# Handing out D^T G one step after the transposes of D in a fused attention, MoE and soft-MoE kernel

## The chip, the cores and the metric

One core of a Trainium2 chip runs the whole program. The metric is device time in microseconds (us), from the start of the program on the core to its end; the median of several runs counts. The profile is that of one execution. It names the engines PE (TensorE, matmuls; PEld is its weight load), DVE (VectorE), ACT (ScalarE), POOL (GpSimd) and SP (SyncE, which here issues the transfers).

## What is computed

Chunked attention, then a squared-relu MLP, then a soft mixture of eight experts, all in float32:

```python
# q, k, v: 8 x 8 x 576 x 64, cut into chunks of 64 rows
attn = softmax(scale * q_c @ k_c.T); x = attn @ v_c     # x: 4608 x 512
h = np.maximum(x @ w_in, 0.0)                           # 4608 x 2048
x = h * h @ w_out                                       # 4608 x 512
logits = x @ phi                                        # 4608 x 32
d = softmax of logits down the 4608 tokens
slot_input = d.T @ x                                    # 32 x 512
slot_out = per expert: relu(slot_input[e] @ w1[e]) @ w2[e]
c = softmax of logits along the 32 slots
return c @ slot_out                                     # 4608 x 512
```

## The kernel before

The 4608 tokens are 36 tiles of 128, grouped into blocks: blocks 0 and 1 with one and two tiles (joined for the later work as "block 1"), and blocks 2 to 12 with three tiles each. A block's work in the middle of the kernel is 16 **steps**, one for each 128 columns of w_in. In step t TensorE computes h for this step (`moe_h`, L727, 12 matmuls), ScalarE takes relu and square, and two steps later (`LAG = 2`) TensorE transposes the result g (`moe_turn`, L761), ScalarE copies it into a buffer G (`moe_keep`, a copy at L188), and after every fourth step TensorE adds to the logits L (`moe_logits`, L778). The transposes of g go to one of two PSUM banks in turn: `gT` for even steps, `L0` for odd ones, once block 2's logits are done.

w_out is applied late: the kernel keeps G, the squared activations with tokens down the partitions, and computes D^T G, where D is the exponential of the logits in the softmax over tokens, with a running maximum. This is the work of `soft(b)`, a generator that starts in the step after the block's last logits. Each `yield` ends its part in one step; `run_gen` puts the next part into the next step. Since a block's last logits fall into step 1 of the block behind it, its parts fall into these steps of the next block:

- step 2: Ls, the logits scaled (L854)
- step 3: their sum over four partial rows (L864)
- step 4: the running maximum, the exponential dts (L874 to L883)
- step 5: `slots_softmax`, the softmax over slots (L896 to L907)
- step 6: the transposes of D (L917, TensorE) and, on VectorE, dd = their product with a scale (L919)
- step 7: D^T G, 24 matmuls of dd with the four G buffers of the block (L926), and on VectorE `acc = acc * al + y` (L937)

Into the same steps `put_until` puts the attention of later tiles, each operation by its stage. Of what stands around step 7 and 8 it is this: in step 8 the scores of the block's third tile (L446 to L448, then on VectorE their maximum L452 and the subtraction L455) and the sum for the scales of another tile (`reduce`, L205 and L206, from three row maxima `am`, L182); in step 9 the product with v of the second tile (L498 to L500). Within a step TensorE's order is attention, h, the part of soft, the transposes of g, the logits.

TensorE executes in this written order (`ST_ORDER = ("PE",)`). For the other engines and for SP the order is made by a scheduler that simulates the program when it is built; each engine's queue then runs in that order.

Buffers that matter here: `misc()` hands out three PSUM banks in turn in the order of the calls, to scores, sums, products with v and the parts of soft alike; a bank can be written anew when its last reader is done. G has a ring of seven buffers (`NG_RING`), taken in the order of first use, four for each block. dd has one buffer. In block 12 the buffers of G that are idle by then are given to the loads of the expert weights at step 9 (`at(u0 + 9, ...)`), and `load_units` issues these loads on SP.

Of the kernel before, what the change touches and what calls it, by code (L numbers as in the profile page):

```python
# [74 lines left out]
def kernel(  # L75
# [95 lines left out]
    def misc():  # L171
        x = bank_of.get(turn[0])
        if x is None:
            while n_misc[0] % 3 in held_banks:
                n_misc[0] += 1
            x = n_misc[0] % 3
            n_misc[0] += 1
        return ps_m.tile([P, 512], F32, tag=f"misc{x}", name="misc")
# [670 lines left out]
    def soft(b):  # L849
        s0, n = blocks[NB if b == 1 else b]  # L850
        last = s0 + n == NT
# [68 lines left out]
            out=dd, in0=tp, in1=iv.unsqueeze(2).to_broadcast([P, n, NS]), op=ALU.mult  # L920
        )
        yield
        y = misc()
        for j in range(n):
            for g in range(NQ):
# [408 lines left out]
    for i in range(9, NT):  # L1334
        b, j = tile_block[i]
# [51 lines left out]
    end = len(steps) + LAG  # L1387
    at(2, lambda: put_rest(2, [("s", NB, x) for x in range(fa, NF)]))
    run_gen(2, soft(1))
    t = min(0, min(slots, default=0))  # L1390
    ctx.enter_context(
        tc.manual_schedule(engines={getattr(mybir.EngineType, e) for e in ST_ORDER})
    )
    while t < end or any(x >= t for x in slots):
        put_rest(t)
        put_until(t + 1)
        b, f = steps[t] if 0 <= t < len(steps) else (None, None)
        if b == 2 and f % QF == 0:
            put_rest(t, [("s", NB, x) for x in range(f, f + QF)])
        if b is not None:  # L1400
            moe_h(b, f)
            moe_relu(b, f)
            moe_square(b, f)
            if (b, f) == (NB - 1, NF - 1):
                give((big, f"xb{b % 2}", 1536))
        for fn in slots.pop(t, []):
            fn()
        if b == NB - 1 and f % 2:
            give((big, f"wi{f // 2}", 1024))
        if 0 <= t - LAG < len(steps):  # L1410
            b, f = steps[t - LAG]
            moe_turn(b, f)
            moe_keep(b, f)
            if f % QF == QF - 1:
                moe_logits(b, f // QF)
            if f == NF - 1:
                if b == NB - 1:
                    give((big, "g0", 1536))
                gen = soft(b)
                run_gen(t + 1 if b < NB - 1 else t, gen)  # L1420
                if b == NB - 1:
                    slots[t].pop()()
        t += 1
# [220 lines left out]
```

## Time and profile before

| | us |
|---|---|
| runs (three) | 777.81, 778.6, 783.45 |
| median of the runs | 778.6 |
| the profiled execution | 778.18 |
| its span in the profile | 776.4 |
| TensorE busy | 707.2 (91%) |
| ScalarE busy | 457.1 (59%) |
| VectorE busy | 431.7 (56%) |
| GpSimd busy | 167.4 (22%) |

The span reaches from the first to the last instruction of the profile. Busy time is the union of an engine's instructions. A wait is idle time of an engine ahead of an instruction, put down to the instruction or transfer that released it.

### The profile page before, as it was taken

The numbers are of one execution on the slowest core, as the hardware profiler recorded it, in microseconds if no ns is written. First come the engines' busy times: TensorE is split into PE (matmuls) and PEld (weight loads), VectorE is DVE, ScalarE is ACT, GpSimd is POOL, SyncE is SP. The second block draws the span as 40 slices with busy tenths as digits, with TensorE's granted clock in tenths as the row PEclk, the third lists the DMA queues.
The fourth block names the chain that finished last, engine by engine and source line by source line (L and its number), as shares of the span: only waits on it lengthen the run. The fifth ranks groups of instructions, "written<-read, shape, count | busy, mean of one in ns | idle before, by whom it ended". The sixth has DMA issues, their size and how long they took to land.

```text
span 776.4 us, 16693 instructions
## 1 busy us (share of the span) xinstructions
PE 707.2 (91%) x6612; PEld 456.1 (59%) x6612; DVE 431.7 (56%) x908; ACT 457.1 (59%) x951; POOL 167.4 (22%) x209
## 2 busy tenths in 40 slices
PE   5788999889999999998999989999999999969790
PEld 4677776665566565665666656656566565524350
DVE  4799996367666565656566566656565301022160
ACT  3688887554666565656676556656566655531150
POOL 3332211131223222223122222322232200030000
PEclk9899999999999999999999999999999999999995
DMA  7896934234364544543544737444567423669998
GB/s 155 215 279 161 217 120 139 66 66 87 81 137 92 98 83 83 123 96 69 109 96 89 100 62 142 86 96 83 82 90 184 150 83 117 227 214 356 349 353 255
DMA packets 242589, 110.47 MB, mean 142 GB/s; under 512 B 201808, under 2 KB 235600, under 8 KB 242512
## 3 DMA queue, kind: packets, MB, share of 16 engines
q1 hardware_dynamic: 242512, 109.41, 58.0%
q8 instruction: 52, 0.85, 0.5%
q14 instruction: 25, 0.20, 0.1%
HBM read 78.71 MB, written 9.44 MB: 114 GB/s over the span
## 4 chain that ended last, share of the span: by engine, by line
PE 65%; DMA 14%; DVE 12%; ACT 3%; issue 2%; SPq 1%; POOL 1%; DVEq 0%; POOLq 0%; ACTq 0%
PE hps L727 38%; PE gT L761 7%; PE L L778 4%; PE misc L926 4%; DMA unit<-in_moe_w_dram 3%; DMA qkT<-qk 3%; DMA qkv<-in_v_dram 2%; PE ehps L1466 2%; DVE qk L276 2%; DMA qkv<-in_q_dram 2%; DMA qkv<-in_k_dram 2%; DMA pT<-p 1%; DVE am L182 1%; DVE vbd L425 1%; DVE stage L281 1%
## 5 line engine op out<-in xcount | busy, mean ns | idle before, releaser
L727 PE MATMUL hps<-xb,wi 128*128 128x384 f16 (+2 forms) x2400 | 407.8, 320 | 0.5 <-ACT g L742 0.2
L727 PEld LDWEIGHTS <-wi 128*128 128x128 f16 x2400 | 224.9, 98 | 138.8 <-issue 17.6
L742 ACT ACTIVATE g<-hps,inv_w 128x384 f32<-128x384 f32 (+1 forms) x200 | 112.7, 563 | 98.4 <-PE hps L727 96.6
L188 ACT ACTIVATE G<-gT 128x384 f32<-128x384 f32 (+1 forms) x200 | 94.2, 471 | 33.8 <-PE gT L761 30.6
L182 DVE TENSOR_REDUCE am<-qkv 128x1 bf16<-128x512 f32 x90 | 61.9, 687 | 83.6 <-DMA qkv<-in_v_dram 31.9
L761 PE MATMUL gT<-ident,g 128*128 128x128 f32 x576 | 98.1, 277 | 4.0 <-ACT G L188 3.1
L749 ACT ACTIVATE g<-g 128x384 f32<-128x384 f32 (+2 forms) x188 | 96.8, 515 | 1.5
L761 PEld LDWEIGHTS gT<-ident,g 128*128 128x128 f32 x576 | 73.0, 144 | 28.8 <-issue 10.4
L420 POOL TENSOR_SCALAR vbd<-qkv,as 64x512 f16<-64x512 f32 x54 | 41.7, 772 | 97.2 <-PE misc L500 81.5
L471 POOL TENSOR_TENSOR ex<-ex,rs 128x512 f32<-128x512 f32 x27 | 29.3, 1085 | 103.4 <-DVE rs L468 93.0
L410 DVE SCALAR_TENSOR_TENSOR qk<-qkv,as,qk 128x512 f16<-128x512 f32 x54 | 39.4, 756 | 20.8 <-ACT qk L405 20.3
L425 DVE SCALAR_TENSOR_TENSOR vbd<-qkv,as,vbd 64x512 f16<-64x512 f32 x54 | 47.3, 876 | 1.0
L405 ACT ACTIVATE qk<-qkv,as 128x512 f16<-128x512 f32 x54 | 36.8, 716 | 10.7 <-DVE as L215 10.7
L778 PE MATMUL L<-g,wp 128*32 128x384 f32 x384 | 41.7, 498 | 0.0
L926 PE MATMUL misc<-G,dd 128*32 128x512 f32 x288 | 33.4, 596 | 7.2 <-DVE dd L919 6.6
L484 POOL TENSOR_TENSOR p<-ex,p 128x512 f16<-128x512 f32 x27 | 34.9, 1292 | 21.7 <-ACT p L481 21.7
L481 ACT ACTIVATE p<-ex 128x512 f16<-128x512 f32 x27 | 17.0, 630 | 35.5 <-POOL ex L471 35.5
L223 POOL TENSOR_SCALAR iv_all<-ai 128x1 f32<-128x1 f32 x27 | 7.5, 276 | 118.5 <-DVE ai L218 117.6
L435 DVE COPY qbd<-qkT 64x1024 f16<-64x1024 f16 x54 | 22.7, 420 | 17.3 <-DMA qkT<-qk 16.5
L510 DVE SCALAR_TENSOR_TENSOR xb<-misc,xb 128x512 f16<-128x512 f32 x27 | 18.1, 671 | 25.1 <-ACT xb L504 24.8
L461 ACT ACTIVATE ex<-ex,es 128x512 f32<-128x512 f32 x27 | 19.4, 718 | 19.4 <-DVE ex L455 19.4
L854 DVE TENSOR_TENSOR Ls<-L,iv_all 128x384 f32<-128x384 f32 x12 | 6.6, 553 | 41.0 <-PE L L778 40.8
(156 smaller groups left out, 1018.7 us busy)
## 6 DMA issues: line engine op xcount, KB each, us to landing
unit<-in_moe_w_dram SPq DMA_DIRECT2D x34, 512.0 KB, 4.5
unit<-in_moe_w_dram SPq DMA_DIRECT2D x60, 256.0 KB, 6.0
qkv<-in_q_dram SPq DMA_DIRECT2D x72, 128.0 KB, 3.4
qkv<-in_k_dram SPq DMA_DIRECT2D x72, 128.0 KB, 3.3
qkv<-in_v_dram SPq DMA_DIRECT2D x72, 128.0 KB, 3.4
stage<-in_moe_w_in_dram SPq DMA_DIRECT2D x16, 512.0 KB, 5.1
stage<-in_moe_w_out_dram SPq DMA_DIRECT2D x16, 512.0 KB, 5.8
out_dram<-o SPq DMA_DIRECT2D x14, 512.0 KB, 6.3
```

The lines of the kernel that those rows point to most:

```text
L182: dve.tensor_reduce(out=am, in_=src, axis=AX.X, op=ALU.max, apply_absolute_value=True)
L188: act.activation(out=out, in_=in_, func=ACTF.Copy)
L405: act.activation(out=qk16[:, 2 * a], in_=flat[:, a], func=ACTF.Copy, scale=v["s"][:, a : a + 1])
L410: dve.scalar_tensor_tensor(out=qk16[:, 2 * a + 1], in0=flat[:, a], scalar=v["s"][:, a : a + 1], in1=qk16[:, 2 * a], op0=ALU.mult, op1=ALU. ...
L420: pool.tensor_scalar(out=dst[0], in0=vin, scalar1=v["s"][pr, 2:3], scalar2=1.0, op0=ALU.mult, op1=ALU.mult,)
L425: dve.scalar_tensor_tensor(out=dst[1], in0=vin, scalar=v["s"][pr, 2:3], in1=dst[0], op0=ALU.mult, op1=ALU.subtract,)
L727: pe.matmul(hp, wi[f][:, wl, kt], xb[:, xl, kt], start=(nm == 0), stop=(nm == 3 * KT - 1))
L742: act.activation(out=g, in_=hp, func=ACTF.Relu, scale=sc)
L749: act.activation(out=g, in_=g, func=ACTF.Square)
L761: pe.transpose(gt_ps[b, f][:, j], g[:, j * P : (j + 1) * P], ident)
L778: pe.matmul(L_ps[g0][NS * x : NS * x + NS, :n], wp[:, QF * q + x], g[:, x, :n], start=(q == 0), stop=(q == NQ - 1), tile_position=(0, NS * x),
L926: pe.matmul(y[NS * g : NS * g + NS], dd[:, j], G_q[b, g][:, j], start=(j == 0), stop=(j == n - 1), tile_position=(0, NS * g), skip_group_c ...
```

## The change

After the transposes of D, `soft` gives up one more step before it hands out D^T G, for every block but block 1 and the last. D^T G and the acc behind it fall into step 8 of the next block, and what else is in steps 7 and 8 stays where it is. The last part of the generator comes one step later as well; it is empty.

```diff
@@ -920,6 +920,8 @@
             out=dd, in0=tp, in1=iv.unsqueeze(2).to_broadcast([P, n, NS]), op=ALU.mult
         )
         yield
+        if not last and b > 1:
+            yield
         y = misc()
         for j in range(n):
             for g in range(NQ):
```

## Rows read from the trace of the kernel before

**Rows 1.** The page: busy us (share) and instructions; busy tenths in forty slices.

```profile
PE 707.2 (91%) x6612; PEld 456.1 (59%) x6612; DVE 431.7 (56%) x908; ACT 457.1 (59%) x951; POOL 167.4 (22%) x209
...
PE   5788999889999999998999989999999999969790
```

**Rows 2.** TensorE's waits: line waited for, us in total, times, longest.

```profile
PE misc L926 <- DVE dd L919: 6.6, 4, 2.0
...
PE gT L761 <- ACT G L188: 3.1, 3, 1.8
```

**Rows 3.** TensorE's timeline (start, length, instruction, [idle before]): D^T G, three blocks.

```profile
457.67 2.78 PE L926 MATMUL misc<-G,dd 128*32 128x512 f32 x24 [1.89 <-DVE dd L919]
...
507.55 2.78 PE L926 MATMUL misc<-G,dd 128*32 128x512 f32 x24 [0.88 <-DVE dd L919]
...
558.33 2.78 PE L926 MATMUL misc<-G,dd 128*32 128x512 f32 x24 [1.79 <-DVE dd L919]
```

**Rows 4.** TensorE's timeline around D^T G of one block, 351 to 363 us.

```profile
351.57 0.37 PE L917 MATMUL misc<-ident,dts 32*128 32x32 f32 x3
351.98 0.55 PE L761 MATMUL gT<-ident,g 128*128 128x128 f32 x3
352.64 2.11 PE L727 MATMUL hps<-xb,wi 128*128 128x384 f16 x12
356.79 2.78 PE L926 MATMUL misc<-G,dd 128*32 128x512 f32 x24 [2.05 <-DVE dd L919]
359.51 0.55 PE L761 MATMUL gT<-ident,g 128*128 128x128 f32 x3
...
360.59 0.17 PE L205 MATMUL misc<-am,ones 128*128 128x3 bf16 x1
...
360.64 2.11 PE L727 MATMUL hps<-xb,wi 128*128 128x384 f16 x12
362.59 0.49 PE L761 MATMUL gT<-ident,g 128*128 128x128 f32 x3
362.92 0.19 PE L498 MATMUL misc<-pT,vbd 128*128 128x64 f16 x1
```

**Rows 5.** VectorE's timeline of the same block, 335 to 363 us.

```profile
335.23 0.69 DVE L182 TENSOR_REDUCE am<-qkv 128x1 bf16<-128x512 f32 x1 [0.33 <-DMA qkv<-in_v_dram]
...
348.88 0.42 DVE L435 COPY qbd<-qkT 64x1024 f16<-64x1024 f16 x1
349.34 0.69 DVE L510 SCALAR_TENSOR_TENSOR xb<-misc,xb 128x512 f16<-128x512 f32 x1
...
352.83 0.26 DVE L900 TENSOR_TENSOR cmat<-misc,cm 128x96 f32<-128x96 f32 x1
355.02 0.69 DVE L182 TENSOR_REDUCE am<-qkv 128x1 bf16<-128x512 f32 x1 [1.93 <-DMA qkv<-in_v_dram]
...
356.49 0.25 DVE L919 TENSOR_TENSOR dd<-misc,iv_all 128x96 f32<-128x96 f32 x1
359.64 0.75 DVE L937 SCALAR_TENSOR_TENSOR acc<-acc,al,misc 128x512 f32<-128x512 f32 x1 [2.90 <-PE misc L926]
360.79 0.69 DVE L452 TENSOR_REDUCE mx<-misc 128x8 f32<-128x512 f32 x1 [0.40 <-PE misc L206]
...
361.53 0.68 DVE L455 TENSOR_TENSOR ex<-misc,mx 128x512 f32<-128x512 f32 x1
```

**Rows 6.** TensorE's timeline at block 1's D^T G.

```profile
178.05 2.78 PE L926 MATMUL misc<-G,dd 128*32 128x512 f32 x24
181.39 0.55 PE L761 MATMUL gT<-ident,g 128*128 128x128 f32 x3 [0.56 <-ACT G L188]
```

**Rows 7.** ScalarE's timeline after block 2's D^T G.

```profile
209.12 0.99 ACT L188 ACTIVATE G<-gT 128x384 f32<-128x384 f32 x2 [1.64 <-PE misc L926]
```

**Rows 8.** Stretches: length, busy (instructions) by engine, clock, DMA share, GB/s.

```profile
660.00:670.00 10.00, 10.00 (x70) 6.25 (x69) 0.00 (x0) 5.49 (x13) 0.00 (x0) 1.00 0.76 270
...
680.00:690.00 10.00, 6.37 (x49) 3.44 (x49) 3.04 (x10) 4.02 (x9) 3.69 (x4) 1.00 0.23 78
```

## The prediction

> **What bounds the kernel now.** I read the page first: its busy shares and its forty slices [rows 1]. TensorE is busy 91% of the span, and its slices stand at 9 nearly without a break from the tenth on; VectorE, the next engine for this change, is busy 56%. The reader is to see a kernel whose middle, about 190 to 675 us, goes at the pace of TensorE's own instruction stream, so only TensorE's idle time can be won there. So I went next to TensorE's waits, longest in total first [rows 2]. The first line is the very instruction that the change moves: the 24 matmuls of D^T G (L926) waited for dd (L919) four times, 6.6 us in all, at most 2.0. The other wait that I need is that of the transposes of g for the copy into G (L761 for L188), 3.1 us in three times.
>
> Then the order of time. TensorE's timeline through one block [rows 4] shows a waiting case: the transposes of D (L917) at 351.57, those of g, the h of step 7, which ends at 354.74, and then nothing until D^T G starts at 356.79, 2.05 late. The other three cases waited 1.89, 0.88 and 1.79 [rows 3]; with the 2.05 that is 6.61. The other six of the ten blocks that the edit touches have no such row: there dd came just in time.
>
> VectorE's timeline of the same block says why dd was late [rows 5]. dd is a short instruction (0.25 us), and its input was there since about 352. But it stands behind a row maximum of v (L182), which waited 1.93 for a transfer until 355.02, and behind the rest of slots_softmax (0.78, from the maximum's end at 355.71 to 356.49). That maximum belongs to a later tile; VectorE's order comes from the scheduler, so a maximum whose load is late holds up whatever stands behind it. After dd VectorE idles 2.90 until D^T G is done and acc (L937) can be added.
>
> **The change part by part.** Nothing is added or removed on any engine: ten times the 24 matmuls and the acc behind them come one step later, and the part issues no transfer. The terms:
>
> *1. The wait for dd.* In the new order TensorE goes from the end of h at 354.74 to the transposes of g, the scores of the next block's third tile, the sum for its scales (L205), the next h, and only then to D^T G. Between the end of D^T G and the end of that h stand today 359.51 to 360.64 (1.13) and 360.64 to 362.59 (1.95) [rows 4], 3.08 together. So D^T G would come at 357.82, and dd ends at 356.74 [rows 5]: 1.08 to spare in the worst of the four cases, more in the others. Term: -6.61.
>
> *2. What is reached earlier.* In those four blocks the scores come up to 2.05 and 2.72 (the length of D^T G, 356.79 to 359.51) earlier than today. Is anything of theirs late? The scores need qbd, whose second copy started at 348.88 and took 0.42; the sum needs three maxima, the last of which was taken at 335.23 [rows 5], twenty microseconds before. Both would be reached after 354.74. Cost 0; without that cover it would be the lateness of either.
>
> *3. The banks.* misc() hands out three banks in turn. Today the order is D^T G, scores, sum, then the p v product of the second tile (L498); after the change it is scores, sum, D^T G, p v. The scores inherit the bank that xl (L510) had left at 350.03, the sum that of slots_softmax, left by L900 at 353.09, D^T G that of the transposes of D, which dd itself has read. The p v product had the bank of D^T G, free once acc has read it; now it has that of the scores, free once L455 has read it. In the new order L452 can start right after dd, at 356.74, and L452 and L455 together took 360.79 to 362.21, 1.42 [rows 5]: free at 358.16. TensorE comes to p v at 357.82 + 2.72 + 0.33 (362.59 to 362.92 today [rows 4]) = 360.87. Cost 0, with 2.71 to spare; what it costs without that cover is the second rival.
>
> *4. The ring of G.* G has seven buffers, handed out in the order of first use. From the third block on, a block's D^T G is read long before its buffers come round: the first reuse is by the copy of step 14 of the next block. In the block after block 2 it is otherwise: the two early groups filled the ring in another order, and that block's second buffer is the first one of block 2. So its copy at step 6 must wait for block 2's D^T G. The trace has this today: the copy waited for the end of L926 and ran at 209.12 [rows 7]. Today no transpose waits for it, since D^T G comes before the transposes that use the other gT bank. One step later the transposes behind D^T G (step 8) need the bank that this copy empties. The same pattern is in the trace once, behind block 1's D^T G: it ended at 180.83, and the transposes started at 181.39, after 0.56 of waiting for the copy [rows 6]. Below, the cost is nothing; above, the two copies in a row, 0.99 [rows 7]. I take 0.56, since that row is the same sequence. Term: +0.56, once. ScalarE's queue is held at that copy some 3 us longer than today, and a relu may stand behind the two copies; TensorE needs that relu's bank only for the second h after D^T G, so at least one h of 1.95 and a p v product lie between, and I put it at 0.
>
> *5. The end.* In the last block the loads of expert weights into the three idle G buffers wait for block 11's D^T G; there it moves by a transpose and an h, some 2.3 us. These loads go through SP in order. The DMA engines have room: 0.76 busy at 660 to 670, 0.23 at 680 to 690 [rows 8], 7.7 idle microseconds in the last of these alone. Cost 0; if the room were not there, 2.3.
>
> A rule of the Trainium skill speaks against term 1: the page "Perfetto Trace Analysis", section Optimization Strategy, takes a gap that repeats on the engine that should be saturated as a possible sign of too few buffers. By that rule the gap would come back at another instruction and the sum would be the time before, as in rival three below. The trace agrees only in part: the gap ends on dd, long after the bank of D^T G was left at 350.03, and shows in four blocks of ten [rows 2, 5].
>
> **Sum.** The profiled execution took 778.18, 1.8 more than its span of 776.4. 778.18 - 6.61 + 0.56 = 772.13. The median of the runs before is 778.6, 0.4 above the profiled execution, so I put 772.5. Bounds of the known terms: 771.9 (no cost of the ring) to 773.0 (0.99 there).
>
> **The rivals.**
>
> *One: dd is later too.* VectorE's order is made anew, and another instruction that waits for a load may come to stand ahead of dd. If that costs one more 1.93 [rows 5], 1.08 of it is covered in the worst blocks and 0.85 is seen; in four blocks 3.4 comes back: 776. For it: such maxima wait often. Against it: up to dd nothing in a block is moved.
>
> *Two, the other side: acc stands in the way.* Today acc follows dd directly on VectorE. If it kept that place, VectorE would stand still from dd until D^T G has ended at 357.82 + 2.72 = 360.54, acc would start 0.13 later as today (359.51 to 359.64 [rows 4, 5]) and take 0.75, then L452 and L455 1.42: the bank of p v would be free at 362.84 and not at 358.16, and TensorE, there at 360.87, would wait 2.0. Nine blocks have this p v: 18 us, 790.5. It decides from 0.7 us a block (6.05 over nine), which is when L452 starts more than 3.4 us after dd. Against it: VectorE's order follows what is ready first (a maximum ran twenty microseconds before the sum that needs it [rows 4, 5]), and the scores will be done by 355.82 (354.74 and 1.08, from 359.51 to 360.59 today [rows 4]), 4.7 us before D^T G has ended.
>
> The rule beside it is in the Trainium skill, page "PSUM — Partial Sum Buffer", section Engine vs sequencer instructions: VectorE's and ScalarE's queues are strictly first in, first out. By it whatever stands behind a waiting acc does wait; the trace agrees, with 2.90 of idle VectorE ahead of acc.
>
> *Three: the wait only moves*, in whole, to another instruction that VectorE is late with, or the order of the other engines changes so that as much is lost elsewhere: 778.6, no change. Against it: I found nothing late behind D^T G.
>
> **How the numbers follow.** Forecast, 772.5: 0.70. One, 776: 0.12. Two, 790.5: 0.07. Three, 778.6: 0.07. The rest, 0.04, is a new order that saves more than the four waits. The forecast's own spread is about 1 us each way, and a measurement of this kernel can tell about 1% from no change, that is below 770.8 or above 786.4. So the gain of 0.8% that I expect lies inside "within 1%"; part of the forecast's spread and the rest lie beyond it. Faster by over 1%: 0.14; within 1%: 0.78; slower: 0.08. The range takes in one and three and leaves out two: 770.0 to 779.5. The forecast alone would be 771.0 to 774.0.
>
> **What would show it.** In the changed kernel's profile: no wait of L926 for dd in TensorE's waits (right) or one of a microsecond in several blocks (rival one). On VectorE L452 and L455 between dd and acc (right) or acc directly behind dd and waits of L498 (rival two). One new wait of L761 for the copy at about 212, around 0.5. A wait of scores or sum for VectorE would refute term 2, and a start of the last phase that is not some 6 us earlier would refute the sum, as would any wait of over a microsecond that is repeated from block to block.

## The result: 1.1% faster

The changed kernel took 771.66 us (median of six runs, 769.53 to 774.87); the kernel before, in the runs beside it, 779.95 (six runs, 777.16 to 784.92). The ratio is 0.9892, with a 95% interval of 0.9861 to 0.9923. 772.5 was predicted. The profile after is of an execution of 774.87, the slowest of the six, with a span of 773.1.

The page of the changed kernel shows nearly the same busy times as [rows 1]; TensorE's is 3.9 higher at a mean granted clock of 0.972 (0.982 before), and none of that lies in the middle of the kernel, as the rows of the first experiment show:

```profile
PE 711.1 (92%) x6612; PEld 457.7 (59%) x6612; DVE 428.1 (55%) x908; ACT 457.3 (59%) x951; POOL 161.9 (21%) x209
...
PE   5788999898999999999999999999999999969790
```

The difference is in TensorE's waits (line waited for, us in total, times, longest). The line of [rows 2] in which D^T G, now L928, waits for dd is gone; the one wait of L928 that is left is in the last block, which the edit leaves out. The waits of the transposes of g have one more case:

```profile
PE gT L761 <- ACT G L188: 3.7, 4, 1.9
...
PE misc L928 <- DVE rs__8963 L936: 0.5, 1, 0.5
```

TensorE's timeline through the block of [rows 4] has no gap. Behind the h of step 7 come the transposes of g, scores and sum, the next h, then D^T G:

```profile
353.05 0.37 PE L917 MATMUL misc<-ident,dts 32*128 32x32 f32 x3
353.44 0.55 PE L761 MATMUL gT<-ident,g 128*128 128x128 f32 x3
354.09 2.11 PE L727 MATMUL hps<-xb,wi 128*128 128x384 f16 x12
356.03 0.49 PE L761 MATMUL gT<-ident,g 128*128 128x128 f32 x3
357.06 0.17 PE L205 MATMUL misc<-am,ones 128*128 128x3 bf16 x1
...
357.12 2.11 PE L727 MATMUL hps<-xb,wi 128*128 128x384 f16 x12
359.15 2.78 PE L928 MATMUL misc<-G,dd 128*32 128x512 f32 x24
361.87 0.55 PE L761 MATMUL gT<-ident,g 128*128 128x128 f32 x3
362.25 0.19 PE L498 MATMUL misc<-pT,vbd 128*128 128x64 f16 x1
```

VectorE's timeline of this block, to compare with [rows 5]: the maximum still waits for its load, 1.74, and dd still ends late, at 358.00. But D^T G starts only at 359.15, so 1.15 are to spare (1.08 were worked out). L452 and L455 run between dd and acc, which waits no more:

```profile
356.28 0.69 DVE L182 TENSOR_REDUCE am<-qkv 128x1 bf16<-128x512 f32 x1 [1.74 <-DMA qkv<-in_v_dram]
...
357.75 0.25 DVE L919 TENSOR_TENSOR dd<-misc,iv_all 128x96 f32<-128x96 f32 x1
357.92 0.68 DVE L452 TENSOR_REDUCE mx<-misc 128x8 f32<-128x512 f32 x1
...
358.65 0.68 DVE L455 TENSOR_TENSOR ex<-misc,mx 128x512 f32<-128x512 f32 x1
...
362.01 0.75 DVE L939 SCALAR_TENSOR_TENSOR acc<-acc,al,misc 128x512 f32<-128x512 f32 x1
```

The one new wait stands behind block 2's D^T G, in TensorE's timeline:

```profile
210.63 2.78 PE L928 MATMUL misc<-G,dd 128*32 128x512 f32 x24
213.97 0.55 PE L761 MATMUL gT<-ident,g 128*128 128x128 f32 x3 [0.56 <-ACT G L188]
```

### The profile page after: what moved, and what is told of

Same layout as the page of the kernel before. It is cut to its first block, busy times and chain, and to the rows that moved or that the text cites. A ratio compares the mean times of both kernels' runs of the same rounds, so it can differ in the third digit from the quotient of the medians.

```text
span 773.1 us, 16704 instructions
## 1 busy us (share of the span) xinstructions
PE 711.1 (92%) x6612; PEld 457.7 (59%) x6612; DVE 428.1 (55%) x908; ACT 457.3 (59%) x951; POOL 161.9 (21%) x209
## 4 chain that ended last, share of the span: by engine, by line
PE 71%; DMA 10%; DVE 9%; ACT 4%; issue 1%; POOL 1%; SPq 1%; DVEq 0%; POOLq 0%; ACTq 0%
PE hps L727 41%; PE gT L761 7%; PE misc L928 4%; PE L L778 4%; DMA unit<-in_moe_w_dram 3%; PE ehps L1468 2%; DVE qk L276 2%; DMA qkT<-qk 2%; DMA qkv<-in_k_dram 2%; DMA qkv<-in_q_dram 1%; PE misc L332 1%; DMA qkv<-in_v_dram 1%; DVE stage L281 1%; PE misc L498 1%; DVE qk L275 1%
## 5 line engine op out<-in xcount | busy, mean ns | idle before, releaser
L420 POOL TENSOR_SCALAR vbd<-qkv,as 64x512 f16<-64x512 f32 x54 | 37.2, 689 | 87.5 <-PE misc L500 71.8
L425 DVE SCALAR_TENSOR_TENSOR vbd<-qkv,as,vbd 64x512 f16<-64x512 f32 x54 | 44.7, 828 | 0.7
L928 PE MATMUL misc<-G,dd 128*32 128x512 f32 x288 | 35.1, 622 | 0.5 <-DVE rs__8963 L936 0.5
```

Of the source, the lines that this page charges most:

```text
L420: pool.tensor_scalar(out=dst[0], in0=vin, scalar1=v["s"][pr, 2:3], scalar2=1.0, op0=ALU.mult, op1=ALU.mult,)
L425: dve.scalar_tensor_tensor(out=dst[1], in0=vin, scalar=v["s"][pr, 2:3], in1=dst[0], op0=ALU.mult, op1=ALU.subtract,)
L928: pe.matmul(y[NS * g : NS * g + NS], dd[:, j], G_q[b, g][:, j], start=(j == 0), stop=(j == n - 1), tile_position=(0, NS * g), skip_group_c ...
```

## The experiments

The theory: the gain is the waits for dd, less the new wait behind block 2. The first rival: there is a gain in every block, from VectorE no longer standing still ahead of acc. For the stretch in which the two differ I take the *middle*, from the start of block 1's D^T G to the start of the last block's transposes of D (178.05 to 684.91 before: 506.86). Two of the expectations below begin it at block 2's D^T G, but that one is moved by the edit itself.

### The same kernel again

No edit.

> The changed kernel once more, beside the kernel before on the same chip. Theory (the gain is the four waits for dd, 6.6 us, less the one new wait behind block 2's D^T G, 0.56): 6 us faster, ratio 0.9925; in the profile no wait of D^T G for dd, the middle (from block 2's D^T G to the last transposes of D) 6 to 7 us shorter. Rival (there is a gain in every block, from VectorE no longer standing still ahead of acc): 8 to 10 us faster, ratio 0.989 or lower, and the blocks without a wait are shorter too, by 0.2 us or more each.

Median 771.96, ratio 0.9891 (0.9857 to 0.9925). No wait for dd in its profile; the middle took 499.26, against 498.84 in the first profile of the change: 7.6 and 8.0 less than the 506.86 before. That is more than the 6 to 7 of the theory, and the ratio is the rival's.

The middle as one stretch (length, busy by engine, granted clock, DMA share, GB/s), in the first profile before and then in the first of the change:

```profile
178.05:684.91 506.86, 492.62 (x4444) 308.54 (x4444) 278.18 (x611) 313.45 (x664) 115.30 (x136) 1.00 0.50 106
```

```profile
180.95:679.79 498.84, 492.09 (x4444) 308.41 (x4443) 273.23 (x607) 314.01 (x664) 110.78 (x135) 1.00 0.50 107
```

TensorE is busy 0.5 less than before; its idle time fell from 14.24 to 6.75, which is 7.5 of the 8.0.

### Only the four blocks that waited, and only the other six

```diff
-        if not last and b > 1:
+        if not last and b in (5, 7, 8, 9):
```

> The later D^T G only in the four blocks that waited before (5, 7, 8 and 9). Theory: the whole of the gain and no wait behind block 2's D^T G: 6.6 us faster, ratio 0.9915. Rival (a gain in every block alike): four tenths of it, about 3 us, ratio 0.996.

```diff
-        if not last and b > 1:
+        if not last and b in (2, 3, 4, 6, 10, 11):
```

> The later D^T G only in the other six blocks (2, 3, 4, 6, 10 and 11). Theory: no gain, and 0.56 us lost behind block 2's D^T G: ratio 1.000 to 1.001; the four waits for dd stand in the profile as before, about 6.6 us in all. Rival (a gain in every block alike): six tenths of it, about 5 us, ratio 0.994.

The four alone: 772.89, ratio 0.9905 (0.9876 to 0.9935), nearly all of the gain. The other six: 780.13, ratio 1.001 (0.9988 to 1.0031), nothing. Their lines in TensorE's waits, first that of the six, then that of the four:

```profile
PE misc L928 <- DVE dd L919: 6.0, 4, 1.8
```

```profile
PE misc L928 <- DVE dd L919: 0.3, 1, 0.3
```

With the six moved the four waits stand where they stood. A gain in every block alike is out: it would have given the six 0.994.

### Block 2 left out

```diff
-        if not last and b > 1:
+        if not last and b > 2:
```

> The later D^T G in all blocks from block 3 on; block 2 as before. Theory: as the changed kernel without the wait of the transposes of g for the copy behind block 2's D^T G, so 0.56 us faster than it in the profile's middle: ratio to before 0.9915. Rival (that wait comes from something other than the ring of G): the wait of 0.56 at about 214 us stays.

Median 771.52, ratio 0.9893 (0.9863 to 0.9922). The wait of the transposes for the copy behind block 2's D^T G is gone, and with it one case of four and 0.7 of the total:

```profile
PE gT L761 <- ACT G L188: 3.0, 3, 1.7
```

So the wait does come from the ring of G. In the time 0.56 can't be told from nothing: the interval is over 4 us wide. The middle, 498.52, is 0.3 and 0.7 below the two profiles of the change.

### dd made later

```diff
-        dve.tensor_tensor(
-            out=dd, in0=tp, in1=iv.unsqueeze(2).to_broadcast([P, n, NS]), op=ALU.mult
-        )
+        for _ in range(5 if not last and b > 1 else 1):
+            dve.tensor_tensor(
+                out=dd, in0=tp, in1=iv.unsqueeze(2).to_broadcast([P, n, NS]), op=ALU.mult
+            )
```

In the kernel before, five times:

> The kernel before with dd computed five times over in the blocks from 2 on (four more instructions of 0.25 us on VectorE ahead of D^T G, the same values). Theory (D^T G comes just when dd is done): each extra 0.7 to 1.0 us is seen in full in the blocks where dd had nothing to spare, eight of ten: 6 to 8 us slower than before, ratio 1.008 to 1.010, and the waits for dd sum to 12 to 15 us. Rival (the waits for dd are a sign of something else that is late): no slower.

In the changed kernel, five times, and nine times with 9 in place of 5:

> The changed kernel with dd computed five times over. Theory: in the changed kernel dd ends 1.0 us or more ahead of D^T G in every block, so the 0.7 to 1.0 us are covered: as the changed kernel, ratio to before 0.990, and no waits for dd over 0.1 us. Rival (VectorE is what sets the pace around D^T G): slower than the changed kernel by what dd costs more, 8 us, ratio 1.000.

> The changed kernel with dd computed nine times over, 1.5 to 2.0 us more. Theory: more than the three tightest blocks have to spare (1.0, 1.15 and 1.22 us), less than the others have (2.3 and more): waits for dd of 0.3 to 1.0 us in three blocks, 1 to 3 us in all, ratio to before 0.992 to 0.994. Rival (VectorE sets the pace): 15 us slower than the changed kernel, ratio 1.01.

Before, the delay is seen: 792.29, ratio 1.0157 (1.0109 to 1.0206). After, the same delay is nearly covered: 773.45, ratio to before 0.9924 (0.99 to 0.9948), with one wait for dd, of 0.2; the middle took 500.32, some 1.3 more than in the changed kernel, and the transposes of D waited once more for the exponential, 0.8. Nine times is more than the cover: 777.2, ratio 0.9969 (0.9943 to 0.9994). The waits of the kernel before with five and of the changed kernel with nine:

```profile
PE misc L927 <- DVE dd L920: 16.6, 8, 3.3
```

```profile
PE misc L929 <- DVE dd L920: 5.0, 5, 1.2
```

Two sizes were off. With nine, five blocks wait and not three, and they wait 5.0 us in all where 1 to 3 were expected: the nine dd together took 2.58, one takes 0.25, so the delay was 2.3 and not 1.5 to 2.0. And the kernel before with five lost 13.7 us where 6 to 8 were expected. The waits rose by 10.0 (6.6 to 16.6; the five dd together took 1.42, so the delay was 1.2 and not 0.7 to 1.0), and something was added to them: after the longest wait, 3.30, the 24 matmuls of D^T G took 4.48 and not 2.78, in TensorE's timeline; and the row of the stretch from 361 to 364 (length, busy by engine, granted clock, DMA share, GB/s) has the clock at 0.56, which is the lower of its two levels, 1.2 GHz, for most of the stretch:

```profile
360.57 4.48 PE L927 MATMUL misc<-G,dd 128*32 128x512 f32 x24 [3.30 <-DVE dd L920]
```

```profile
361.00:364.00 3.00, 3.00 (x20) 0.78 (x16) 0.00 (x0) 0.00 (x0) 0.00 (x0) 0.56 0.00 0
```

That profile has three such stretches in its middle, each after a wait for dd (3.30, 2.48 and 3.27). Their D^T G took 4.48, 4.40 and 4.48, 5.0 more than three times 2.78; with the 10.0 that is 15.0, and the middle grew by 14.8 (521.66 for 506.86).

### Two steps later

```diff
-        if not last and b > 1:
+        if not last and b > 2:
             yield
+            yield
```

> D^T G two steps later instead of one, in the blocks from 3 on, block 2 as before. Theory: nothing is left to gain, the waits for dd being gone with one step: the same as one step later without block 2, ratio 0.989 to 0.992. Rival (more room, more gain): another 3 us or more, ratio 0.986 or lower.

Median 772.99, ratio 0.9915 (0.9887 to 0.9942): nothing more than with one step.

### slots_softmax out of the way

```diff
-        if not last:
+        early = last or b == 1
+        if not last and early:
             slots_softmax(misc()[:, : n * NS])
+        if not last:
             yield
...
             out=acc, in0=acc, scalar=al, in1=y, op0=ALU.mult, op1=ALU.add
         )
+        if not early:
+            yield
+            slots_softmax(misc()[:, : n * NS])
```

(The step that slots_softmax had stays, empty.)

> The kernel before with D^T G where it was, in step 7, but slots_softmax moved from step 5 to the step behind D^T G in the blocks from 2 on, so that its instructions no longer stand between the late maximum and dd on VectorE. Theory (dd is late by the load that the maximum waits for, 1.9 us, and by the rest of slots_softmax behind it, 0.8): the four waits shrink by about 0.8 us each, from 6.6 to 3 to 4 us in all; ratio 0.995 to 0.997. Rival (dd is late by its own input, or by what is ahead of the maximum): the waits stay, ratio 1.000.

Median 779.02, ratio 0.9981 (0.9957 to 1.0005), nearly nothing, where the theory had 0.995 to 0.997. On VectorE dd now stands directly behind the late maximum:

```profile
355.62 0.69 DVE L182 TENSOR_REDUCE am<-qkv 128x1 bf16<-128x512 f32 x1 [2.09 <-DMA qkv<-in_v_dram]
356.22 0.25 DVE L921 TENSOR_TENSOR dd<-misc,iv_all 128x96 f32<-128x96 f32 x1
```

D^T G waits 0.89 in this block where it waited 2.05, but 5.2 in all, in six blocks, and not the 3 to 4 expected. And the transposes of D now wait for the exponential in three blocks more than before, as here, and give part of the gain back:

```profile
352.47 0.37 PE L919 MATMUL misc<-ident,dts 32*128 32x32 f32 x3 [0.72 <-ACT dts L877]
...
356.52 1.92 PE L928 MATMUL misc<-G,dd 128*32 128x512 f32 x16 [0.89 <-DVE dd L921]
```

In this block the load that comes late is the larger part of dd's lateness, as the rows said; shortening the chain behind it isn't enough. No run took the maximum itself, or its load, out of dd's way.

### The kernel before, three more profiles

The open point after the first experiments was the size: 6.6 of waits removed, but 7.4 to 8.3 gained. The second rival: the first profile showed fewer waits than an execution has.

> The kernel before once more, for a second profile. Theory (the gain is the waits for dd that one execution shows): waits for dd in the same four blocks, 6 to 7 us in all, the middle (from block 2's D^T G on) within 0.5 us of the first profile's. Rival (the first profile showed fewer waits than an execution has on average, which is why the gain by the median is over 6 us): 8 us or more of waits.

> The kernel before, a third profile. Theory (dd's lateness differs between executions, since it hangs on when loads arrive; the first profile, 6.6 us in four blocks, was a low one): the waits for dd sum to 7 to 9 us in six blocks or more, the middle 2 to 4 us longer than in the first profile. Rival (the second profile was the odd one): 6 to 7 us in the same four blocks.

> The kernel before, a fourth profile, on the same terms: 7 to 9 us of waits for dd in six blocks or more by the theory, 6 to 7 us in the same four blocks by the rival.

Beside more runs of the same kernel the second stands at 782.17, ratio 1.0017 (0.9982 to 1.0052); the third and the fourth are single executions, of 780.66 and 776.55. The second, third and fourth profile of the kernel before have these lines among TensorE's waits, where [rows 2] has 6.6 in four cases:

```profile
PE misc L926 <- DVE dd L919: 8.0, 7, 2.1
```

```profile
PE misc L926 <- DVE dd L919: 8.6, 7, 2.1
```

```profile
PE misc L926 <- DVE dd L919: 7.1, 6, 1.9
```

The mean of the four is 7.6; the first was the lowest. And in two of the four, after the longest wait, D^T G ran at the lower clock. The second profile's timeline with its stretch from 460 to 464, and below it the third's with its stretch from 457 to 461; the granted clock is 0.58 in both:

```profile
460.60 4.48 PE L926 MATMUL misc<-G,dd 128*32 128x512 f32 x24 [2.11 <-DVE dd L919]
```

```profile
460.00:464.00 4.00, 3.40 (x17) 0.82 (x21) 0.51 (x3) 0.00 (x0) 0.00 (x0) 0.58 0.01 4
```

```profile
456.43 4.22 PE L926 MATMUL misc<-G,dd 128*32 128x512 f32 x24 [2.12 <-DVE dd L919]
```

```profile
457.00:461.00 4.00, 4.00 (x26) 1.00 (x17) 0.30 (x1) 0.00 (x0) 0.00 (x0) 0.58 0.02 4
```

The first profile, with waits of up to 2.05, kept the full clock there, and so did the fourth, with up to 1.89. Neither profile of the changed kernel has such a stretch between the two ends of its middle. The middles of the four are 506.86, 510.50, 507.76 and 505.94, 507.8 in the mean; those of the change 498.84 and 499.26, 499.1. The difference is 8.7. The waits came as the theory of these runs had them, the middles did not: the third was to be 2 to 4 longer than the first and is 0.9 longer, and the fourth is 0.9 shorter.

## Why the prediction came out as it did

**The wait for dd (term 1)** was the right mechanism: the four blocks alone bring the gain, the other six nothing, and a dd made later costs 13.7 before and hardly anything after. Its size is what was off: -6.61 was read from one execution. The prediction takes dd as just in time in the other six blocks. In the first profile that holds for four of them, blocks 2, 3, 4 and 6, where D^T G starts 0.05 to 0.13 behind the end of dd; blocks 10 and 11 have 1.09 and 2.06 to spare. A load that comes a little later makes a wait out of the first kind: blocks 3, 4 and 6 are the three more that wait in the second and the third profile. The maximum ahead of dd waited 1.66, 1.57 and 1.83 for its load there in the first profile, and 1.85, 1.75 and 2.38 in the second. By four profiles the waits are 7.6 in the mean, and 1.7 and 1.44 more at the lower clock in two of the four, 0.8 in the mean: 8.4. With the 0.56 against it that makes 7.8. From 779.95, the median of the kernel before beside the result, it leads to 772.1, from 779.37, beside the repeat, to 771.6; measured were 771.66 and 771.96. The price of a wait was taken as its length; that a long one can slow the work behind it was not in the sum.

That 772.5 lies as near as 0.8 to the measured 771.66 is in part luck. The forecast gain was 6.1, the measured one 8.3; of the 2.2 between them 1.35 was made up by the start, since the sum began at 778.6 and the kernel before took 779.95 in the runs beside the result.

**What is reached earlier, and the banks (terms 2 and 3)** cost nothing that was seen, as worked out. Neither scores nor sum wait for VectorE in the blocks that were moved (a sum waits for its maximum at 185.01, 0.50, in the second profile of the change, and at 188.08, 0.81, in the first before, both ahead of block 2's D^T G). The one p v product that waits for L455, 0.16 at 437.87 in the second profile, stands 32 us behind block 6's D^T G and not next to it. L455 ended at 359.33 (358.65 and 0.68), 2.92 ahead of the p v product at 362.25; 2.71 had been worked out.

**The ring of G (term 4)** was right to the digit: one wait, 0.56, at 213.97, and with block 2 left out it is gone. It was read from the same sequence at block 1 [rows 6].

**The end (term 5)**: block 11's D^T G moved by a transpose and an h, and the last phase took no longer for it that could be seen: from the last transposes of D to the end of the span 91.5 in the second profile of the change and 91.5 in the first before. In the first profile of the change it took 93.3, of which 1.7 is the last block's D^T G at the lower clock (4.48). The room for the loads stands in [rows 8].

**The start of the last phase**, to be some 6 us earlier: the last transposes of D start at 679.79 and 674.54, 5.1 and 10.4 earlier than before. Most of that spread lies ahead of the first block that was moved, since block 1's D^T G started at 180.95 and 175.28 (178.05 before); from there on it is 8.0 and 7.6.

**Rival one** (dd later too) did not come: the smallest room between dd and its D^T G in the changed kernel's two profiles is 1.01 and 1.30. **Rival two** (acc in the way) did not come: in VectorE's new order acc stands behind L452, L455 and eight more, which fits the argument that this order follows what is ready first. What it would have cost wasn't tried. **Rival three** (the wait only moves) is what happened in part where slots_softmax was moved instead, not here. The rule of the Trainium skill, page "Perfetto Trace Analysis", section Optimization Strategy, that a repeated gap may mean too few buffers, did not hold for this gap: it was gone with one step and no buffer more.

The **chances** put 0.78 on "within 1%"; the measured 1.1% lies just beyond, with an interval on both sides of the line. That follows in the main from the size of term 1.

About 0.9 of the 8.7 in the middle is in no term (8.4 - 0.56 = 7.8). TensorE's other listed waits there sum to 7.24, 7.90, 5.14 and 6.71 in the four profiles before and, without the new 0.56, to 5.69 and 6.47 in the two after: 0.7 less in the mean, but they differ by more than that between executions of one kernel, so it stays open.

## What to carry to other kernels

Where one engine sets the pace in a written order, put other work between a hand-over and its user when the hand-over hangs on something that arrives at uneven times; one step was enough here, and two brought no more. Read a wait that hangs on transfers from more than one execution before it is used as a term, and look at the matmuls behind it: a long wait can also cost clock. Before a user is moved, go through every ring that it holds; the only cost here was found by counting seven buffers.

## What the runs showed of the hardware that I had not expected

After a wait of 2.11, 2.12 or 3.30 us of a TensorE that had been busy, the granted clock fell to its lower level while the next matmuls ran, and 24 matmuls that take 2.78 took 4.48, 4.22 and 4.48. After the waits for dd of up to 2.05 in the four profiles of the kernel before it stayed up. But the length of the wait doesn't settle it. Ahead of the middle, in the first profile of the change, the clock fell after a wait of 1.55; TensorE's timeline and the stretch from 177 to 179:

```profile
175.54 1.33 PE L661 MATMUL misc<-pT,vbd 128*64 128x64 f32 x32 [1.55 <-DVE cmat L900]
```

```profile
177.00:179.00 2.00, 2.00 (x27) 1.50 (x25) 1.05 (x2) 0.59 (x1) 0.00 (x0) 0.50 1.14 223
```

And of two waits of 2.48 in the kernel before with five dd, one was followed by the lower clock and one was not; and the same wait of 2.79 for the exponential in the last block was followed by it in the first profile of the change (the clock's mean is 0.57 from 681 to 685) and not in the first of the kernel before (1.00 from 685 to 689). The rows of these two stretches, the change first:

```profile
681.00:685.00 4.00, 4.00 (x24) 0.78 (x16) 0.17 (x1) 0.00 (x0) 0.72 (x2) 0.57 0.00 0
```

```profile
685.00:689.00 4.00, 3.50 (x32) 1.35 (x33) 1.43 (x6) 0.04 (x1) 1.75 (x3) 1.00 0.00 0
```
